# First keys gathered in four quadrants, their mask and weight applied behind the turn; GpSimd's set-up as scheduled tasks; the low weight bits extracted on ScalarE

## The chip, the cores and the metric

The program runs on one core of a Trainium2 chip. The metric is device time in microseconds (us) of one execution, the median of several runs. The engines are named as the profile names them: PE (TensorE: matmuls; PEld its weight loads), DVE (VectorE), ACT (ScalarE), POOL (GpSimd), SP (SyncE, which here only issues DMAs).

## The reference, cut to what matters

Linear attention with a delta rule over 768 tokens for 4 x 8 heads of 48, then two feed-forward layers over 3072 tokens. All in float32.

```python
k_n = k / (np.linalg.norm(k, axis=-1, keepdims=True) + 1e-06)
for t in range(S):                       # state: B, H, 48, 48
    y[:, :, t] = einsum('bhd,bhde->bhe', q[:, :, t], state)
    v_old = einsum('bhde,bhd->bhe', state, kt)
    state = state + bt[:, :, :, None] * einsum('bhd,bhe->bhde', kt, vt - v_old)
x = y.transpose(0, 2, 1, 3).reshape(3072, 384)
h = x @ w_in                             # 384 -> 2048
x = (h * sigmoid(1.702 * h)) @ w_out     # 2048 -> 384
p = domain_probs / domain_probs.sum(-1, keepdims=True)
out = sum(p[:, e:e+1] * (np.maximum(x @ w1[e], 0) @ w2[e]) for e in range(4))
```

## The kernel before, in words

**Attention.** The 768 steps are cut into 12 chunks u of 64 tokens. For a chunk all 32 heads lie in 16 groups g, two heads side by side (x = 0, 1) on the upper and lower half of the 128 partitions. Inside a chunk the recurrence becomes a triangular system in blocks of SB = 32 tokens: matmuls of the keys with themselves give `ps`; `keep_d` takes its diagonal blocks times a mask (and the rates beta) into `GG`, `keep_x` the blocks beside them into `G`. A triangular inverse is worked out for two chunks at a time (w = 0, 2, ..., 10): `begin` turns `GG` into `X` with a 32x32 transpose, `step(j)` eliminates column by column, `to_rows` turns it back. For w = 0 (`queue_first_inverse`) this is done on DVE, on two diagonal halves of 16 that `turn`, `first`, `out1`, `second`, `out2` join with matmuls; for all later w (`queue_inverse`) it is done on POOL. `queue_chain` then runs the chunk: `ks`, `rest`, `solve`, `cross`, `read` (the output y), `write` (the new state).

**First feed-forward layer.** The tokens are in 6 tiles t of 512; tile t needs chunks 2t and 2t+1. For each of 16 slices f of the hidden layer PE does 9 matmuls into `ph` (layer 1, L1013), ACT the gelu and its high part, DVE the low part `gh` (L1126), PE 9 matmuls into `px` (layer 2, L1108), one f later. The tiles 0 and 1 start in halves of 256 tokens. Weights and activations are split into a high and a low float32r part, so each product takes 3 matmuls. The weights w of this layer come as 64-bit numbers, and their float32 words are put together on chip in tile 0, per f: `small` (ACT L286), `low` (three low bits moved down, DVE L289), `shift` (DVE L293), `hi` (ACT L298), `lo` (DVE L301). Buffer `raw` or `rw` holds one f's words; PE waits for `wdone[f]` in tile 0.

**The second layers** (4 experts, L1013, L1235, L1265) follow from 613 us on; the change does not touch them.

**Order.** Each engine runs its instructions in the order in which the program was written out, and that order is made by a planner (`Order`, `Task`): every piece of the attention is a task with an engine, an estimated cost, dependencies and a priority; the planner keeps a clock for each engine (`od.clk`) and writes out a task when its estimate says that it is ready, between the matmuls of the feed-forward layer (`tick`). The estimate of a step of the inverse on POOL is `(0.52 + 0.0037 * m)` times 1.5 for w = 2, times 1.0 for later w. What really has to wait is ordered by semaphores; a wrong estimate makes an engine wait, or leaves a piece late. Before the first matmul of layer 1 only attention of chunk 0 and the first weights are there to do: a chain through all engines, called the start here.

**Set-up.** POOL writes masks (`gmask`, `cmask`, `pmask`, `hmask`) and zeros (`PQ`, `SU`, `stage`) ahead of all tasks, and the planner's clock of POOL starts at 9.5 us.

Of the kernel before, what the change touches and what calls it, by code (L numbers as in the profile page):

```python
# [9 lines left out]
I32 = mybir.dt.int32  # L10
AF = mybir.ActivationFunctionType
# [13 lines left out]
GW = 1  # L25
# [125 lines left out]
def delta_attention_moe_moe_kernel(  # L151
# [55 lines left out]
    cmask = ap_.tile([128, SB], F32, name="cmask")  # L207
# [43 lines left out]
    def queue_w1(f, after):  # L251
# [111 lines left out]
    NR = {}  # L363
# [88 lines left out]
    def queue_q(u):  # L452
# [8 lines left out]
        lq = task(load, "HW", 1.32, (edone.get(u - 2), normed[u] if u > 1 else None), lat=4.8, prio=p if u < 4 else p - 30, slack=5)  # L461
        ends, visits, masks = [], [], []
        whole = 1 if u < 2 else 2
        for o in range(2):
# [18 lines left out]
            if len(visits) == whole:  # L483
                t = task(lambda fs=tuple(visits): weave(fs), "PE", 1.0 if whole == 1 else 1.3,
                         (*placed[u], lq, begun[0], *(ends[-1:] if u > 1 else ())), prio=p + 1,
                         can=lambda: None if u > 1 and not od.moe else some_free(banks(), whole))
                for c, f in masks:
                    c.setdefault("end", []).append(task(f, "DVE", 0.6, (t,), prio=p + 1))
                    ends.append(c["end"][-1])
# [16 lines left out]
    def queue_premask(us):  # L506
# [11 lines left out]
        premasked[w] = task(premask, ("POOL", "DVE"), (1.2 * len(us), 0.6 * len(us)), (normed[w],), prio=p,  # L518
# [4 lines left out]
    def queue_g(u):  # L523
# [6 lines left out]
        whole = 1 if u < 4 else 2  # L530
        for o in range(2):
# [3 lines left out]
            def gram(o=o, cell=cell, flip=flip):  # L535
# [4 lines left out]
                for i in range(8):  # L540
                    g = 2 * i + o
                    if u < GW:
                        for x in range(2):
                            d, r = DR[x], TR[x]
                            mm(ps[r:r + C, i, :], lhsT=kr[d:d + D, g, :], rhs=kr[d:d + D, g, :], start=True, stop=True)
                            yield
                        continue
# [10 lines left out]
            def keep_d(x, o=o, cell=cell, flip=flip):  # L558
                if w not in GG:
                    GG[w] = scr[claim(SCR, gheld[w]["end"])][:, 0:2 * NP * SB].rearrange("p (g i) -> p g i", i=SB)  # L560
                a = rows(o)[0]
                if u < GW:
# [15 lines left out]
            halves.append((cell, gram, keep_d, keep_x))  # L578
# [5 lines left out]
            for hc, _, kd, kx in halves:  # L584
                parts = range(2) if whole == 2 and hc is not first else (None,)
                diag += [task(lambda kd=kd, x=x: kd(x), "DVE", 0.4 if u >= GW else 1.2, (a, premasked.get(w)), prio=p,
                              can=None if w or u or hc is not first else lambda: any_free(SCR)) for x in parts]
# [9 lines left out]
    def queue_inverse(us):  # L597
# [46 lines left out]
    def queue_first_inverse(us):  # L644
# [733 lines left out]
```

## Time and profile before

| | |
|---|---|
| median of 3 runs | 1409.41 us (1405.75 to 1409.59) |
| profiled execution | 1406.45 us, its span 1404.7 us |
| busy in the span | PE 1354.4 us (96%), DVE 617.5 (44%), ACT 421.2 (30%), POOL 202.5 (14%) |
| PE idle or waiting | mostly ahead of 66.4 us, where layer 1 starts, and in a few places up to 336 us |

The span is the time from the first to the last instruction of the program; 1.75 us of the profiled execution lie outside it. Shares of the whole span say little here: the start, tile 0, the step from tile 0 to tile 1 and the rest have different limits, so the profile is read by stretch.

### The profile page before, as it was taken

What the parts mean: (1) busy time and instruction counts of PE and PEld (TensorE: products, weight loads), DVE (VectorE), ACT (ScalarE), POOL (GpSimd) and SP (SyncE); (2) the same over time, 40 slices, a digit from 0 to 9 for tenths busy, and PEclk for the clock granted to TensorE, in tenths of its full rate; (3) what the DMA queues carried; (4) which work ended last, traced back from release to release, by engine and by line L of the source; (5) the groups of instructions that cost most, each with busy time, mean ns of one, the idle gap of its engine ahead of it and who ended that gap; (6) DMA issues with size and microseconds to landing.
All of it is one profiled execution on the core that took longest, in us unless ns stands there. A gap on an engine that the chain in (4) does not pass through costs nothing.

```text
span 1404.7 us, 29499 instructions
## 1 busy us (share of the span) xinstructions
PE 1354.4 (96%) x13072; PEld 1144.5 (81%) x13072; DVE 617.5 (44%) x1035; ACT 421.2 (30%) x797; POOL 202.5 (14%) x355
## 2 busy tenths in 40 slices
PE   5699999998999999999999999999999999999998
PEld 4588789986878788878888888888888888888888
DVE  7879466474363423323333224443233433233343
ACT  2564344352342434422222112222122222111111
POOL 3057543603507200000000000000000000000000
PEclk9999989999999999999999999999999999999999
DMA  8550131222020103201100001010001000011111
GB/s 222 171 173 17 28 96 40 61 62 61 12 61 7 39 5 134 68 0 29 33 30 30 8 1 30 31 38 31 1 19 30 31 31 8 0 30 31 31 30 46
DMA packets 53696, 63.39 MB, mean 45 GB/s; under 512 B 37120, under 2 KB 38592, under 8 KB 53568
## 3 DMA queue, kind: packets, MB, share of 16 engines
q1 hardware_dynamic: 53568, 61.50, 15.4%
q8 instruction: 102, 1.67, 0.5%
q14 instruction: 26, 0.21, 0.1%
HBM read 52.58 MB, written 7.91 MB: 43 GB/s over the span
## 4 chain that ended last, share of the span: by engine, by line
PE 92%; DVE 4%; issue 2%; DMA 1%; ACT 1%; SPq 0%; DVEq 0%; ACTq 0%
PE ph L1013 42%; PE po L1235 23%; PE px L1108 14%; PE po L1265 5%; PE y L849 2%; PE ch L820 1%; PE gp L550 1%; PE ch L806 1%; PE ch L872 1%; PE ch L835 1%; PE gp L473 1%; DMA rw<-in_w_dram 1%; DMA k<-in_k_dram 0%; ACT su L183 0%; DMA kt<-in_kt_dram 0%
## 5 line engine op out<-in xcount | busy, mean ns | idle before, releaser
L1013 PE MATMUL ph<-xs,w 128*128 128x512 f32 (+1 forms) x2808 | 657.5, 377 | 3.6 <-ACT xs L183 2.0
L1013 PEld LDWEIGHTS ph<-xs,w 128*128 128x128 f32 x2808 | 504.1, 190 | 96.7 <-ACT xs L183 2.1
L1296 DVE SCALAR_TENSOR_TENSOR hh<-ph,hh 128x512 fp32r<-128x512 f32 x192 | 132.5, 690 | 503.4 <-ACT hh L1295 503.4
L1235 PE MATMUL po<-hh,w 128*128 128x512 f32 x1440 | 352.4, 389 | 0.0
L1235 PEld LDWEIGHTS po<-hh,w 128*128 128x128 f32 x1440 | 270.4, 188 | 56.0
L1295 ACT ACTIVATE hh<-ph 128x512 fp32r<-128x512 f32 x192 | 114.9, 598 | 616.6 <-PE ph L1013 616.6
L1108 PE MATMUL px<-gh,w 128*128 128x512 f32 (+1 forms) x1080 | 231.6, 354 | 2.3 <-DVE gh L1126 2.1
L1108 PEld LDWEIGHTS px<-gh,w 128*128 128x128 f32 x1080 | 177.3, 190 | 30.4 <-DVE gh L1126 3.0
L1126 DVE TENSOR_TENSOR gh<-ph,gh 128x512 fp32r<-128x512 f32 (+1 forms) x120 | 69.9, 582 | 149.0 <-ACT gh L1125 147.8
L1123 ACT ACTIVATE ph<-ph 128x512 f32<-128x512 f32 (+1 forms) x120 | 59.6, 497 | 184.9 <-PE ph L1013 179.8
L621 POOL TENSOR_TENSOR scr<-scr,itmp 128x30 f32<-128x30 f32 (+9 forms) x150 | 85.0, 567 | 11.8
L619 POOL TENSOR_TENSOR itmp<-scr 128x30 f32<-128x30 f32 (+9 forms) x150 | 80.4, 536 | 11.1
L1265 PE MATMUL po<-w,hh 128*128 128x384 f32 x384 | 73.9, 342 | 0.0
L1265 PEld LDWEIGHTS po<-w,hh 128*128 128x128 f32 x384 | 69.3, 188 | 2.4
L1125 ACT CAST gh<-ph 128x512 fp32r<-128x512 f32 (+1 forms) x120 | 60.2, 502 | 3.8
L183 ACT COPY su<-ch 64x384 f32<-64x384 f32 (+2 forms) x85 | 38.1, 458 | 49.9 <-PE ch L820 48.5
L1095 DVE TENSOR_TENSOR xs<-x,xs 128x512 fp32r<-128x512 f32 x72 | 45.3, 684 | 0.0
L1094 ACT CAST xs<-x 128x512 fp32r<-128x512 f32 x72 | 39.7, 619 | 0.0
L813 DVE TENSOR_TENSOR v<-v,ch 128x384 f32<-128x384 f32 (+1 forms) x56 | 30.1, 551 | 17.5 <-PE ch L835 5.1
L478 DVE TENSOR_TENSOR pq<-gp,pmask 64x512 f32<-64x512 f32 x48 | 33.1, 689 | 5.9 <-PE gp L473 5.1
L243 DVE TENSOR_TENSOR w<-raw,w 128x768 fp32r<-128x768 f32 x32 | 30.7, 958 | 10.3 <-ACT w L242 9.5
L768 POOL TENSOR_TENSOR v<-v,nr 128x768 f32<-128x768 f32 x9 | 13.3, 1479 | 127.2 <-DMA v<-in_v_dram 119.1
(118 smaller groups left out, 765.8 us busy)
## 6 DMA issues: line engine op xcount, KB each, us to landing
raw<-in_we_dram SPq DMA_DIRECT2D x32, 384.0 KB, 3.0
rw<-in_w_dram SPq DMA_DIRECT2D x14, 768.0 KB, 5.7
raw<-prd SPq DMA_DIRECT2D x20, 256.0 KB, 3.2
kt<-in_kt_dram SPq DMA_DIRECT2D x24, 192.0 KB, 5.1
k<-in_k_dram SPq DMA_DIRECT2D x12, 384.0 KB, 6.1
pq<-in_q_dram SPq DMA_DIRECT2D x24, 192.0 KB, 4.2
v<-in_v_dram SPq DMA_DIRECT2D x12, 384.0 KB, 3.1
out_dram<-oacc SPq DMA_DIRECT2D x80, 48.0 KB, 1.7
```

The costliest lines, as they stand in the source:

```text
L619: E.tensor_tensor(out=tv, in0=x[:, j:j + 1, j + 1:].broadcast_to([128, m, r]), in1=x[:, 0:m, j:j + 1].broadcast_to([128, m, r]), op=ALU.mult)
L621: E.tensor_tensor(out=x[:, 0:m, j + 1:], in0=x[:, 0:m, j + 1:], in1=tv, op=ALU.add)
L1013: mm(ps, lhsT=w[:, a, kk * 128:(kk + 1) * 128], rhs=xs[kk][:, b, cs], start=kk == 0 and i == 0, stop=kk == KD - 1 and i == 2)
L1095: nc.vector.tensor_tensor(out=s[:, 1, :], in0=src, in1=s[:, 0, :].bitcast(F32), op=ALU.subtract)
L1108: mm(px[d][:, cs], lhsT=w[:, a, 384 + d * 128:384 + (d + 1) * 128], rhs=gh[:, b, 0:cs.stop - cs.start], start=f == 0 and i == 0 and cs.sta ...
L1123: a = task(lambda: nc.scalar.activation(out=ph, in_=ph, func=AF.Gelu_apprx_sigmoid), "ACT", 0.05 + 0.43 * c, (pe,), **kw)
L1125: a = task(lambda: nc.scalar.copy(out=hi, in_=ph), "ACT", 0.05 + 0.43 * c, (a,), **kw)
L1126: a = task(lambda: nc.vector.tensor_tensor(out=lo, in0=ph, in1=hi.bitcast(F32), op=ALU.subtract), "DVE", 0.07 + 0.53 * c, (a,), **kw)
L1235: mm(po[kk], lhsT=w[:, a, 384 + kk * 128:384 + (kk + 1) * 128], rhs=hh[:, c, :], start=f == 0 and i == 0, stop=f == F2 - 1 and i == 2)
L1265: mm(ps, lhsT=hh[:, a, b * 128:(b + 1) * 128], rhs=w[:, c, 384:768].rearrange("p (k a i) -> p a k i", a=4, k=KD), start=f == 0 and i == 0, ...
L1295: nc.scalar.activation(out=hh[:, 0, :], in_=ph, func=AF.Relu)
L1296: nc.vector.scalar_tensor_tensor(out=hh[:, 1, :], in0=ph, scalar=0.0, in1=hh[:, 0, :].bitcast(F32), op0=ALU.max, op1=ALU.subtract)
```

## The change

1. **Keys of chunks 0 and 1.** All chunks now gather their diagonal blocks by the same four kinds of matmul (32 rows each), so chunk 0 has 32 matmuls more, which are 64 in the profile's count, as a float32 product counts twice there. For w = 0 the diagonal blocks are copied as they are (`keep_raw`, ACT or DVE). The mask and the rates are applied behind the turn: POOL makes `m`, mask times rates, in two products (`weigh`), and `clear` multiplies by it, with one more memset. `cmask` goes.
2. **Set-up.** POOL's eight pieces become tasks of the planner in a new order (`j`, `q0`, `pm`, `h`, `su`, `st`, `q1`, `g`), and the DMAs of q wait for theirs only. The masks' sources lie in `spare`. On SP the loads of `raw` and of the first `rw` stood behind q of chunk 0 and of chunk 1, which both wait for POOL's zeros; now chunk 1's q stands behind these loads.
3. **Low bits.** `low` runs on ACT as an activation (a scaled copy between 32-bit integers) instead of DVE's shift: 16 instructions.
4. **Estimates.** A step of the inverse on POOL is estimated at 1.2 for w = 2 and 0.95 for later w; some others are changed in small ways. The order of all tasks is made anew.

```diff
-            nc.vector.tensor_scalar(out=cell["lo"], in0=cell["lo"], scalar1=29, scalar2=None,
-                                    op0=ALU.logical_shift_right)
+            nc.scalar.activation(out=cell["lo"].bitcast(U32), in_=cell["lo"].bitcast(U32), func=AF.Copy, scale=2.0 ** -29 * (1 - 2.0 ** -16),
+                                 bias=7.5 * 2.0 ** -16 - 0.5)
...
-            b = task(low, "DVE", 0.6, (dep, begun[0]), **kw)
+            b = task(low, "ACT", 0.9, (dep, begun[0]), **kw)
...
-                if u < GW:
-                    for r in range(0, 128, SB):
-                        V.tensor_tensor(out=GG[w][r:r + SB, o:NP:2, :] if not u else GG[w][r:r + SB, NP + o:2 * NP:2, :], in0=cell["ps"][r:r + SB, :, r % C:r % C + SB],
-                                        in1=cmask[r:r + SB].unsqueeze(1).broadcast_to([SB, 8, SB]), op=ALU.mult)
-                    return
...
+                copy(e, GG[w][r:r + n, c * NP + o:(c + 1) * NP:2, :], cell["ps"][s:s + n, :, a:a + SB])
...
-            last = task(lambda j=j: step(j), "POOL", (0.52 + 0.0037 * m) * (1.5 if w == 2 else 1.0), (last,), prio=p)
+            last = task(lambda j=j: step(j), "POOL", (0.52 + 0.0037 * m) * (1.2 if w == 2 else 0.95), (last,), prio=p)
...
+        def weigh(e):
+            bt = BT[w].rearrange("p (h i) -> p h i", h=2)
+            cell["m"] = spare[:, H * H:3 * H * H].rearrange("p (h a b) -> p h a b", h=2, a=H)
+            for h in range(2):
+                (V if e == "DVE" else nc.gpsimd).tensor_tensor(
+                    out=cell["m"][:, h], in0=jmask, in1=bt[:, h].unsqueeze(1).broadcast_to([128, H, H]), op=ALU.mult)
...
-            V.tensor_tensor(out=x, in0=x, in1=bt.unsqueeze(2).broadcast_to([128, 2, H, H]), op=ALU.mult)
+            V.tensor_tensor(out=x, in0=x, in1=cell["m"], op=ALU.mult)
             V.memset(X[w][:, H:, 0:H], 0.0)
+            V.memset(X[w][:, 0:H, H:], 0.0)
...
+        last = task(weigh, ("POOL", "DVE"), (1.2, 0.9), (normed[w], zeros["j"]), prio=0)
+        last = task(clear, "DVE", 1.4, (begun[w], last), prio=p)
```

What it does to the order is shown at three places. First DVE between the rates of chunks 0 and 1 (row `bt`, the reciprocal is ahead of it) and the first step of the inverse; `scr_99` before and `scr_98` after are `GG`, `scr_101` and `scr_100` are `X`. Before:

```order
20 L432 TENSOR_TENSOR bt<-bt,scr_98 128x32
21 L433 STREAM_TRANSPOSE bt<-bt 128x32
22 L564 TENSOR_TENSOR scr_99<-gp,cmask 32x8x32 x4
23 L571 TENSOR_TENSOR scr_99<-gp,cmask 128x8x32
24 L660 STREAM_TRANSPOSE scr_101<-scr_99 128x1024
25 L267 MEMSET rw 128x1
26 L666 TENSOR_TENSOR scr_101<-scr_101,bt 128x2x16x16
27 L667 MEMSET scr_101 128x16x16
28 L668 MEMSET scr_101 128x32
```

After:

```order
19 L433 TENSOR_TENSOR bt<-bt,scr_97 128x32
20 L434 STREAM_TRANSPOSE bt<-bt 128x32
21 L656 STREAM_TRANSPOSE scr_100<-scr_98 128x1024
22 L266 MEMSET rw 128x1
23 L668 TENSOR_TENSOR scr_100<-scr_100,sp 128x2x16x16
24 L669 MEMSET scr_100 128x16x16
25 L670 MEMSET scr_100 128x16x16
26 L671 MEMSET scr_100 128x32
```

The five masked products between the rates and the turn are gone (two plain copies stand further up, ahead of the second reduction), and one memset is new.

Second ACT from the first weights to the copy `out1` of the first inverse (`scr<-gp 128x16x16`), L286 before and L285 after being `small`, L288 after being `low`. Before:

```order
7 L286 ACTIVATE raw<-raw 128x768
8 L286 ACTIVATE rw<-rw 128x768 x3
9 L393 ACTIVATE scr_98<-k_2_83 128x768
10 L183 COPY scr_100<-gp 128x16x16
11 L286 ACTIVATE rw<-rw 128x768
12 L183 COPY su<-ch_593 32x4x48 x4
```

After:

```order
12 L288 ACTIVATE raw<-raw 128x768
13 L288 ACTIVATE rw<-rw 128x768
14 L285 ACTIVATE rw<-rw 128x768
15 L288 ACTIVATE rw<-rw 128x768
16 L285 ACTIVATE rw<-rw 128x768
17 L288 ACTIVATE rw<-rw 128x768
18 L394 ACTIVATE scr_97<-k_2_83 128x768
19 L183 COPY scr_99<-gp 128x16x16
```

Four activations for the low bits now stand ahead of the copy for which PE waits.

Third DVE around `to_rows` of w = 2 (`128x32x32`), which must wait for POOL; L571 before and L558 after are `keep_d` of w = 4, `gh` are the low parts of tile 0's gelu. Before:

```order
194 L1126 TENSOR_TENSOR gh<-ph,gh 128x512
195 L514 TENSOR_TENSOR scr_101<-gmask,bt 128x1024
196 L571 TENSOR_TENSOR scr_101<-gp,scr_101 128x8x32
197 L571 TENSOR_TENSOR scr_101<-gp,scr_101 64x8x32 x2
198 L183 COPY g<-gp 32x8x32
199 L1126 TENSOR_TENSOR gh<-ph,gh 128x512
200 L571 TENSOR_TENSOR scr_101<-gp,scr_101 128x8x32
201 L571 TENSOR_TENSOR scr_101<-gp,scr_101 64x8x32 x2
202 L610 STREAM_TRANSPOSE scr_99<-scr_101 128x1024
203 L1126 TENSOR_TENSOR gh<-ph,gh 128x512 x2
204 L642 STREAM_TRANSPOSE scr_98<-scr_98 128x32x32
```

After:

```order
175 L515 TENSOR_TENSOR scr_100<-gmask,bt 128x1024
176 L1139 TENSOR_TENSOR gh<-ph,gh 128x512
177 L558 TENSOR_TENSOR scr_100<-gp,scr_100 128x8x32
178 L558 TENSOR_TENSOR scr_100<-gp,scr_100 64x8x32 x2
179 L558 TENSOR_TENSOR scr_100<-gp,scr_100 128x8x32
180 L558 TENSOR_TENSOR scr_100<-gp,scr_100 64x8x32 x2
181 L1139 TENSOR_TENSOR gh<-ph,gh 128x512
182 L638 STREAM_TRANSPOSE scr_99<-scr_99 128x32x32
183 L606 STREAM_TRANSPOSE scr_98<-scr_100 128x1024
184 L1139 TENSOR_TENSOR gh<-ph,gh 128x512
```

Counted from the first `gh` of tile 0, `to_rows` of w = 2 stood behind the 21st and now stands behind the 18th of the tile's 24, still behind the `keep_d` of w = 4. With it chunk 2's chain moves: on PE its first matmuls (`ks`) stood behind 14 of tile 0's 16 f and now stand behind 11.

## Rows read from the trace of the kernel before

**Rows 1.** The page: busy time of each engine; DMA queues (packets, MB, share).

```profile
PE 1354.4 (96%) x13072; PEld 1144.5 (81%) x13072; DVE 617.5 (44%) x1035; ACT 421.2 (30%) x797; POOL 202.5 (14%) x355
...
q8 instruction: 102, 1.67, 0.5%
```

**Rows 2.** Busy by stretch: PE, PEld, DVE, ACT, POOL, clock, DMA, GB/s.

```profile
70.00:115.00 45.00, 43.89 (x1004) 40.03 (x1003) 36.15 (x59) 29.09 (x62) 27.61 (x37) 1.00 0.53 150
...
117.70:121.10 3.40, 3.40 (x18) 3.40 (x17) 3.40 (x5) 1.46 (x3) 3.17 (x4) 0.50 0.00 0
...
170.90:175.70 4.80, 1.45 (x70) 1.05 (x73) 1.66 (x3) 1.89 (x4) 4.29 (x7) 1.00 0.48 102
175.70:186.00 10.30, 9.40 (x232) 8.16 (x233) 4.54 (x8) 4.29 (x10) 9.06 (x15) 0.50 0.39 119
...
336.20:1404.70 1068.50, 1063.59 (x6581) 887.53 (x6580) 391.72 (x599) 272.33 (x474) 69.52 (x125) 1.00 0.10 29
```

**Rows 3.** Timeline of DVE in the start: start, duration, line, operation.

```profile
11.03 1.61 DVE L408 TENSOR_SCALAR scr<-scr 128x32 int32<-128x32 int32 x1
...
16.15 1.68 DVE L564 TENSOR_TENSOR scr<-gp,cmask 32x256 f32<-32x256 f32 x4
...
18.32 1.94 DVE L660 STREAM_TRANSPOSE scr<-scr 128x1024 f32<-128x1024 f32 x1
...
21.44 0.27 DVE L667 MEMSET scr<- 128x256 f32 x1
...
54.27 0.18 DVE L408 TENSOR_SCALAR scr<-scr 128x32 int32<-128x32 int32 x1
```

**Rows 4.** Timeline of POOL: last set-up piece; two steps and the end of w = 2.

```profile
10.80 1.81 POOL L1046 MEMSET pq<- 128x2048 f32 x1
...
93.76 1.11 POOL L619 TENSOR_TENSOR itmp<-scr 128x184 f32<-128x184 f32 x1
...
124.58 0.54 POOL L619 TENSOR_TENSOR itmp<-scr 128x184 f32<-128x184 f32 x1
...
132.75 1.92 POOL L625 TENSOR_TENSOR scr<-scr,bt 128x1024 f32<-128x1024 f32 x1
```

**Rows 5.** The chain of waits in the start: start, length, what.

```profile
33.22 1.94 PE gp L718 x128
...
36.19 0.61 PE gp L727 x29
36.80 2.73 issue
```

**Rows 6.** Timeline of SP's DMA queue in the start: start, duration, issues.

```profile
6.24 7.66 SPq L459 DMA_DIRECT2D pq<-in_q_dram  x4
...
14.62 0.43 SPq L277 DMA_DIRECT2D raw<-in_w_dram  x1
```

**Rows 7.** Timeline of ACT in the start; in brackets its idle time before, and why.

```profile
34.12 0.90 ACT L286 ACTIVATE rw<-rw 128x768 f32<-128x768 f32 x1 [0.97 <-DMA rw<-in_w_dram]
...
35.77 0.37 ACT L183 COPY scr<-gp 128x256 f32<-128x256 f32 x1
```

**Rows 8.** Groups by line, the low bits: busy us, mean ns of one | idle before.

```profile
L289 DVE TENSOR_SCALAR rw<-rw 128x768 int32<-128x768 int32 x14 | 9.8, 697 | 0.0
```

**Rows 9.** Timeline of PE in tile 0, around a wait for `gh`.

```profile
117.04 1.54 PE L1108 MATMUL px<-gh,w 128*128 128x256 f32 x8 [1.91 <-DVE gh L1126]
```

**Rows 10.** Timeline of DVE in tile 0: the 18th `gh`; `to_rows` of w = 2.

```profile
132.88 0.65 DVE L1126 TENSOR_TENSOR gh<-ph,gh 128x512 fp32r<-128x512 f32 x1
...
149.59 2.23 DVE L642 STREAM_TRANSPOSE scr<-scr 128x1024 f32<-128x1024 f32 x1
```

**Rows 11.** The chain of waits, later pieces.

```profile
111.24 0.58 DVE rw L289
...
174.27 2.33 DMA stage<-scr
...
325.93 4.84 issue
```

More of the change, by code (lines that the diff above doesn't have):

```diff
@@ L361, in delta_attention_moe_moe_kernel @@
     direct = {}
-    NR = {}
+    NR, zeros = {}, {}
+    spare = wp.tile([128, 1536], F32, name="sp", tag=f"w{RAW - 1}")
+    jmask = spare[:, 0:SB * SB // 4].rearrange("p (a b) -> p a b", a=SB // 2)
     def queue_keys(us):
@@ L487, in queue_q @@
                 for c, f in masks:
-                    c.setdefault("end", []).append(task(f, "DVE", 0.6, (t,), prio=p + 1))
+                    c.setdefault("end", []).append(task(f, "DVE", 0.69, (t, zeros["pm"]), prio=p + 1))
                     ends.append(c["end"][-1])
@@ L529, in queue_g @@
         diag, cross, halves, first = [], [], [], None
[L530 removed]
+        whole = 1 if u in (2, 3) else 2
         for o in range(2):
@@ L585, in queue_g @@
                 parts = range(2) if whole == 2 and hc is not first else (None,)
-                diag += [task(lambda kd=kd, x=x: kd(x), "DVE", 0.4 if u >= GW else 1.2, (a, premasked.get(w)), prio=p,
-                              can=None if w or u or hc is not first else lambda: any_free(SCR)) for x in parts]
+                diag += [task(lambda kd=kd, x=x: kd(x), "DVE", 0.4, (a, premasked.get(w)), prio=p) if w else
+                         task(lambda e, kd=kd, x=x: kd(e, x), ("ACT", "DVE"), (0.42, 0.42), (a,), prio=p,
+                              can=None if u or hc is not first else lambda: any_free(SCR)) for x in parts]
                 cross += [task(lambda e, x=x, kx=kx: kx(e, x), ("ACT", "DVE"), (0.3, 0.33), (a,), prio=p + 1)
@@ L689, in queue_first_inverse @@
                 marks.append(last)
-            last = task(lambda j=j: step(j), "DVE", 0.26 + 0.0042 * j * (H - 1 - j), (last,), prio=p)
+            last = task(lambda j=j: step(j), "DVE", 0.4 + 0.003 * j * (H - 1 - j), (last,), prio=p)
         last = task(end, "DVE", 0.6, (last,), prio=p)
@@ L746, in queue_first_inverse @@
                 a = task(lambda gn=gn, second=second: second(gn), "PE", 1.1 * n / NP, (a,), prio=p)
-            invdone[u] = task(out2, "DVE", 0.41, (a,), prio=p)
+            invdone[u] = task(out2, "DVE", 0.47, (a, *zeros.values()), prio=p)
             ends.append(invdone[u])
@@ L1039, in delta_attention_moe_moe_kernel @@
-        nc.gpsimd.memset(PQ[0], 0.0)
-        for r in range(0, 128, SB):
-            for o in range(2):
-                nc.gpsimd.affine_select(out=pmask[r:r + SB, o], in_=m2[r:r + SB], pattern=[[1, C]], compare_op=ALU.is_gt,
-                                        fill=0.0, base=-(r % C ^ SB * o), channel_multiplier=-1)
-        nc.gpsimd.memset(SU, 0.0)
-        nc.gpsimd.memset(stage, 0.0)
-        nc.gpsimd.memset(PQ[1], 0.0)
-        od.clk["POOL"] = 9.5
+        H = SB // 2
+        E_ = nc.gpsimd
@@ new lines, in delta_attention_moe_moe_kernel, with set_j, set_g @@
+        ones, minus = spare[:, 1024:1024 + C], spare[:, 1024 + C:1024 + C + SB]
+        def set_j():
+            E_.memset(minus, -1.0)
+            E_.affine_select(out=jmask, in_=minus[:, 0:1].unsqueeze(2).broadcast_to([128, H, H]), pattern=[[-1, H], [1, H]],
+                             compare_op=ALU.is_gt, fill=0.0, base=0, channel_multiplier=0)
+        def set_g():
+            for r in range(0, 128, SB):
+                at = slice(r, r + SB)
+                E_.affine_select(out=gmask[at], in_=minus[at], pattern=[[-1, SB]], compare_op=ALU.is_gt,
+                                 fill=0.0, base=0, channel_multiplier=1)
@@ new lines, in set_h, with set_p @@
+        def set_h():
+            E_.memset(hmask, -1.0)
+            for r in range(0, 128, SB):
+                at = slice(r, r + SB)
+                E_.affine_select(out=hmask[at], in_=hmask[at], pattern=[[0, 1]], compare_op=ALU.is_ge,
+                                 fill=0.0, base=H - 1, channel_multiplier=-1)
+        def set_p():
+            E_.memset(ones, 1.0)
+            for r in range(0, 128, SB):
+                for o in range(2):
+                    E_.affine_select(out=pmask[r:r + SB, o], in_=ones[r:r + SB], pattern=[[1, C]], compare_op=ALU.is_gt,
+                                     fill=0.0, base=-(r % C ^ SB * o), channel_multiplier=-1)
@@ L1050, in delta_attention_moe_moe_kernel @@
+        for n, fn, cost in (("j", set_j, 0.5), ("q0", lambda: E_.memset(PQ[0], 0.0), 1.85), ("pm", set_p, 1.95),
+                            ("h", set_h, 0.9), ("su", lambda: E_.memset(SU, 0.0), 1.4),
+                            ("st", lambda: E_.memset(stage, 0.0), 1.4), ("q1", lambda: E_.memset(PQ[1], 0.0), 1.85),
+                            ("g", set_g, 1.1)):
+            zeros[n] = task(fn, "POOL", cost, (), prio=2)
+        od.clk["POOL"] = 0.8
         loaded = queue_tile(0)
```

45 lines of the change are left out of this document (12 added, 33 removed).

## The prediction

> **What bounds the kernel now.** The first view is the page's busy time: PE is busy 96% of the span [rows 1]. The second is busy time by stretch: behind 336 us PE works 1063.59 of 1068.50 us at full clock [rows 2], so nothing that this change does there can shorten the run; it can only lose. What can be won lies before. There the chain of waits and the timelines, read one after the other, show four places where PE stands still for a cause that the change touches: the start, until layer 1 begins at 66.4; a stall in tile 0 that ends at 117.04; the step from tile 0 to tile 1 (170.9 to 186.0); and a pause at 325.93 in which PE waits for nothing that the profile shows. The reader should also see in [rows 2] what follows each stall: the granted clock is 0.50 in 117.7 to 121.1 and in 175.7 to 186.0, the lower of its two levels (1.2 of 2.4 GHz). PE had just stood still both times. Such a stretch costs half of its busy time on top of the stall, and both go together if the stall goes.
>
> **Term 1, from the rates to the turn: −3.3 us.** Behind the last operation on the rates DVE makes four masked products of 1.68 in all and a fifth, and the turn starts at 18.32 instead of 16.15 [rows 3]. The plain copies that replace them stand ahead of the rates, where DVE and ACT wait for keys anyway: −2.17. The first operation on the rates, L408, took 1.61, and 0.18 when it came again [rows 3]; it ended with POOL's last memset (10.80 + 1.81 = 12.61) [rows 4], so I read it as held up by POOL. In the changed order q1, that memset, is not the last piece, and the small selects of `g` stand behind it; POOL reaches them near 11: −1.43, and 0 if the hold stays. One memset of 0.27 is new. Sum −3.33; bounds −1.9 and −3.6 (the memset may overlap its neighbours). `weigh` needs the rates, as the turn does; it is two POOL products of 256 elements, and the nearest row is 1.92 for 1024 [rows 4], so about 0.5 each, 1.0 together. The turn's 1.94 [rows 3] hides it; without that cover it costs up to 1.0. The 64 extra matmuls stand in front of the turn, where PE then waits 11 us for it, and cost nothing.
>
> **Does the gain get through ACT?** The copy `out1`, for which PE's next matmuls wait, ran at 35.77, though PE was done at 33.22 + 1.94 = 35.16 [rows 5]: ACT came from `small`, which had waited for weights until 34.12 [rows 7]. If these weights come no earlier, two `low` of about 0.90 (the price of `small`, the same shape on the same engine, [rows 7]) put `out1` at about 36.7, and all of term 1 is lost. But the weights move. SP spent 7.66 us on four issues of q, as chunk 1's q waits for POOL's zeros until 12.61, and `raw` was issued only at 14.62 [rows 6]. Now `raw` and the first `rw` stand ahead of that wait and can go some 6 us earlier, and what follows them in the queue gains at least part of it. I take it that they land as much earlier as the turn ends.
>
> **Term 2, from the turn's end to `out2`: −1.0 us.** ACT's two extra `low` ahead of `out1` cost up to 1.8, about 0.6 beyond what the earlier weights give back. Against that stands the wait of 2.73 which came 29 matmuls into L727 [rows 5] and waits for no engine. The page gives its cause: 1.67 MB in 102 packets on the instruction queue, 16 KB each, against 2 x 13072 PE instructions [rows 1], 256 to a packet, or 128 matmuls with their weight loads. The boundary of such a block fell 29 into L727, with 128 matmuls of L718 just ahead that went by in 1.94 [rows 5]: too fast for the next block. With 64 more matmuls ahead, this boundary falls 29 + 128 − 64 = 93 into L718 (L722 now), and its block has PE's long wait for the turn to arrive in. The next falls 93 into L731, behind the wait for `out1`. If it is there in time, 2.73 goes; if it comes as late as now, nothing. I take 1.6 of it: −1.6 + 0.6 = −1.0, bounds −2.7 and +1.8. The Trainium skill (Runtime: NRT & Kernel Launch, section Instruction fetch mechanics) has the same blocks, 16 KiB of 256 instructions, and says that the next is fetched while the current one runs, so that the cost of a boundary is mostly hidden. By that rule the shift would give nothing and this term would be +0.6; the 2.73 in the trace speaks against it here.
>
> **Term 3, from `out2` to layer 1: 0.** DVE loses some six `low` of 0.70 [rows 8] and ACT gains as many of 0.90 [rows 7]. In this stretch the chain runs through ACT in its first half and through DVE in its second, so one loses what the other wins. Bounds −2 and +2 (three `low` on either).
>
> **Term 4, tile 0: −3.6 us.** PE waits 1.91 for `gh` [rows 9]. On the chain to it stand three `low`, of which [rows 11] has one; at 0.70 each [rows 8] they are 2.1 of DVE. Without them `gh` comes 2.1 earlier, and the stall is gone with the half-clock stretch behind it, 3.40 / 2 = 1.70 [rows 2]. −1.91 − 1.70 = −3.6; bound 0, where another piece fills DVE's time or ACT's hold the gelu up.
>
> **Term 5, from tile 0 to tile 1: −8.95 us.** `to_rows` of w = 2 ran on DVE at 149.59 [rows 10], though POOL had been done since 132.75 + 1.92 = 134.67 [rows 4]: the planner's factor of 1.5 had put it behind the 21st `gh`. Behind it came chunk 2's chain, whose `stage` transfer of 2.33 at 174.27 [rows 11] is what PE waited for. Of 170.9 to 175.7 PE used 1.45 of 4.80, and then it worked 9.40 of 10.30 at half clock [rows 2]. Lost: 4.80 − 1.45 = 3.35 and 10.30 − 9.40 / 2 = 5.60. In the changed order `to_rows` stands behind the 18th `gh`, which ran at 132.88 [rows 10] and would, moved by terms 1, 2 and 4, run near 125. Is POOL done by then? Two steps of the same 184 elements took 1.11 and 0.54 [rows 4]; the first met a `low` on DVE. Seven of them met POOL's inverse, so without them it should be shorter by some 7 x 0.57 = 4.0: 134.67 − 4.3 − 4.0 = 126.4. So DVE would wait about 1 us there at most, the 19th `gh` is still in time, and chunk 2's matmuls, behind 11 f instead of 14, come over 10 us earlier, where under 5 were missing. −8.95; bound 0.
>
> **Term 6, the pause at 325.93: 0.** 4.84 without a releaser [rows 11] has the look of the block wait of term 2, with some half-clock work behind it, which I put at the 1.7 of term 4. It comes where key loads burst into the DMA queues. In the changed order the matmuls on chunk keys shift against tile f's, and the blocks by 64 matmuls. Neither sign is likelier, so 0, with bounds of −6.5 and +6.5 (it goes, or a second one comes).
>
> **The sum.** −3.3 − 1.0 + 0 − 3.6 − 8.95 + 0 = −16.9. The profiled execution took 1406.45 (a span of 1404.7 and 1.75 outside): 1389.6. It lies 3.0 below the median of 1409.41; I add half of that, as the profile is one of the same spread: 1391.
>
> **The rivals.**
>
> *A. DVE stands in `to_rows` and waits for POOL.* All that DVE has behind it waits too: the transpose of the next `keep_d`, the 19th `gh`, and PE for that. If POOL gains nothing from the missing `low` it ends at 130.4, 5 us behind the 18th `gh`; with 2.23 for `to_rows` [rows 10] and as much for the transpose, the 19th `gh` comes some 3 us late: 3 + 1.7 of half clock, 4.7 in all. The next chunk's pieces move with it, and a second such stall is likely: 1396 with one, 1400 with two. For it: DVE's other operations of 768 elements hold POOL just as well, so POOL's gain is uncertain. Against it: two equal steps at 1.11 and 0.54.
>
> *B. ACT becomes the bound.* It gets 11 `low` of 0.90 in tile 0, where it was busy 29.09 of 45 [rows 2]; 10 us more make 39. A gelu behind them delays `ph` and `gh`, and each such stall costs, as at 117.04, 1.91 + 1.70 = 3.6. With terms 1, 2 and 5 at −13.3 the change loses from the fourth such stall on; with six, −13.3 + 21.6 = +8.3, near 1417. Against it: the average leaves ACT free a seventh of the time, and DVE is lighter by 0.70 for each.
>
> *C. The change does nothing that shows.* What the start and the steps give back is waited for elsewhere: the weights come no earlier (term 1 lost), POOL's chain sets chunk 2 as before, and a second block wait (+6.5) eats term 4 and a part of the rest: 1405 to 1413.
>
> *D. The rule of hidden block waits.* If the 2.73 has another cause that stays, only term 2 changes: −16.9 + 1.6 = −15.3, near 1392.5, inside the likeliest's range. By the Trainium skill's page named at term 2 this would be the time.
>
> **How the numbers follow.** The sum's way 0.48 and D with it 0.12, together the likeliest: 1391; its terms' bounds are mostly independent (term 6 is the widest), and its own range is 1383 to 1398. A 0.20, 1394 to 1405. C 0.12. B 0.08. From 1381 to 1407 leaves out B, most of C and a tail below: some 0.2. A difference under 0.3% (4.2 us) is about what cannot be told from no change here. Faster by more: the likeliest and most of A, 0.77; within: most of C and the rest of A, 0.14; slower: B and a little of C, 0.09.
>
> **What would show it in the profile after.** Term 1: L409 at 0.18, the turn near 15, `begin`'s multiply right behind it without a wait for POOL. Through ACT: `small` of the fourth weights near 31, `out1` within 1 us of PE's end. Term 2: no wait inside L731, or one at its 93rd matmul. Start as a whole: first `ph` 62 to 63. Term 4: no PE wait for `gh` near 110, no half-clock stretch. Term 5: `to_rows` of w = 2 near 127 with POOL done before it, PE without a gap or half clock between tiles 0 and 1. Term 6: where PE waits with no releaser behind 186. What would make the forecast wrong most: DVE standing in `to_rows` for POOL, ACT late with gelu, or a new pause like that of 325.93, with its half-clock stretch.

## The result and the profile after

The changed kernel takes 1387.4 us (1384.29 to 1390.42), the kernel before 1409.5: a ratio of 0.9848, interval 0.9819 to 0.9877. Two more series on other chips gave 0.9825 (0.9802 to 0.9849) and 0.9849 (0.9823 to 0.9875). The profiled execution took 1390.42, the slowest of its series, with a span of 1388.7.

The page and busy time by stretch, after (columns as in [rows 1, 2]):

```profile
PE 1344.4 (97%) x13136; PEld 1133.8 (82%) x13136; DVE 608.6 (44%) x1015; ACT 431.3 (31%) x811; POOL 206.5 (15%) x353
...
q8 instruction: 103, 1.69, 0.5%
```

```profile
70.00:115.00 45.00, 40.52 (x794) 36.62 (x793) 33.21 (x51) 30.10 (x59) 30.64 (x43) 0.96 0.43 124
...
167.00:190.00 23.00, 23.00 (x433) 20.70 (x432) 17.26 (x28) 11.39 (x27) 11.08 (x20) 1.00 0.58 144
```

The step from tile 0 to tile 1 has no gap and no half clock any more (23.00 of 23.00 at 1.00). But in the stretch 70 to 115 PE is busy for less time than in [rows 2]: 40.52 instead of 43.89.

The start, DVE, SP and ACT (timelines, as [rows 3, 6, 7]):

```profile
10.99 0.18 DVE L409 TENSOR_SCALAR scr<-scr 128x32 int32<-128x32 int32 x1
...
14.61 0.21 DVE L434 STREAM_TRANSPOSE bt<-bt 128x32 f32<-128x32 f32 x1
16.54 1.95 DVE L656 STREAM_TRANSPOSE scr<-scr 128x1024 f32<-128x1024 f32 x1 [1.72 <-ACT scr L183]
```

```profile
4.05 1.38 SPq L460 DMA_DIRECT2D pq<-in_q_dram  x2
...
6.16 1.26 SPq L276 DMA_DIRECT2D raw<-in_w_dram  x1
```

```profile
30.91 0.90 ACT L285 ACTIVATE rw<-rw 128x768 f32<-128x768 f32 x1
...
33.36 0.37 ACT L183 COPY scr<-gp 128x256 f32<-128x256 f32 x1
```

The rates end at 14.82, early as forecast, but DVE then waits 1.72 for ACT's copies of the keys, and the turn starts at 16.54. The weights come about 3 us earlier (`small` at 30.91 against 34.12) and `out1` 2.4 earlier (33.36 against 35.77). Why the copies are late is seen on PE, whose timeline and chain of waits follow (`issue` is time in which PE waits for nothing that the profile shows, called a wait without a releaser below):

```profile
14.60 0.21 PE L549 MATMUL gp<-kt 48*32 48x32 f32 x1 [5.11 <-issue]
```

```profile
33.78 1.46 PE gp L731 x93
35.24 1.50 issue
...
72.92 2.72 issue
```

PE waits 5.11 in the middle of chunk 1's keys with no releaser, 1.50 behind exactly the 93rd matmul of L731, and 2.72 at 72.92. The pause at 325.93 is gone. Tile 0 and the step (POOL and DVE timelines, PE's, SP's):

```profile
81.14 0.15 POOL L609 MEMSET scr<- 128x32 f32 x1 [23.48 <-DVE scr L606]
...
127.11 1.92 POOL L621 TENSOR_TENSOR scr<-scr,bt 128x1024 f32<-128x1024 f32 x1
```

```profile
132.64 0.69 DVE L1139 TENSOR_TENSOR gh<-ph,gh 128x512 fp32r<-128x512 f32 x1
133.25 2.20 DVE L638 STREAM_TRANSPOSE scr<-scr 128x1024 f32<-128x1024 f32 x1
```

```profile
105.79 1.22 PE L1121 MATMUL px<-gh,w 128*128 128x256 f32 x8 [1.11 <-DVE gh L1139]
```

```profile
154.26 4.10 SPq L979 DMA_DIRECT2D stage<-scr  x6
```

POOL ends at 129.03, `to_rows` runs at 133.25 right behind the 18th `gh`, and the `stage` transfers go out at 154 instead of around 172.

To see where time went, the losses of PE are summed by stretch of its own progress: idle time plus busy time times (1 − granted clock), over windows of 0.5 us. The start is the time of layer 1's tenth matmul; tile 0 goes to its 180th (12 of tile 0's 16 f), the step to its 288th (a quarter into tile 1), then come the stretch to the 648th, where tile 2 ends, and that to the end of the first feed-forward layer, behind the 1080th. What is left of the span, PE's work and some 3 to 4 us of idle time in the second layers, is 1310 to 1314 us in all kernels.

| kernel | start | tile 0 | step | to 648 | to the second layers | span |
|---|---|---|---|---|---|---|
| before | 68.9 | 5.8 | 9.7 | 8.4 | 0.9 | 1404.7 |
| changed, first profile | 63.6 | 7.7 | 0.1 | 5.8 | 1.1 | 1388.7 |
| changed, second (c0) | 63.3 | 2.1 | 0.1 | 2.2 | 1.1 | 1379.8 |
| changed, third (c1) | 63.2 | 3.2 | 0.1 | 5.7 | 1.0 | 1384.4 |

Between executions of one program it is waits without a releaser that come and go: at 72.92 and 207.67 in the first profile, neither in the second, at 203.27 alone in the third. With them come stretches of half clock (76.5 to 80.0 and 209.6 to 213.1 in the first profile). Another such stretch, where layer 1 begins, stands in the first and the third profile (62.9 to 66.3 and 61.9 to 65.4) and not in the second.

What these waits are can be read from the packets of the instruction queue, which the trace holds one by one: 16 KB each, a block of 128 matmuls with their weight loads. In the first profile one runs from 12.15 to 13.27, and PE goes on at 14.60; another from 34.33 to 35.26, and PE goes on at 36.74. In the kernel before one runs from 328.24 to 329.33, in the pause at 325.93, and PE goes on at 330.77. In all 14 profiles together some 90 waits without a releaser of 0.35 us or more stand where such a block ends in PE's program, about 128 matmuls apart, and each ends 1.2 to 1.6 us after a packet of this queue has landed. So PE waits for its own instructions there. (A wait of 0.70 or 0.71 us at L824, L820 before, stands in every kernel and is not one of them.)

### The profile page after: what moved, and what is told of

The parts are those of the page before. It is cut to its first block, busy times and chain, and to the rows that moved or that the text cites. A ratio compares the mean times of both kernels' runs of the same rounds, so it can differ in the third digit from the quotient of the medians.

```text
span 1388.7 us, 29634 instructions
## 1 busy us (share of the span) xinstructions
PE 1344.4 (97%) x13136; PEld 1133.8 (82%) x13136; DVE 608.6 (44%) x1015; ACT 431.3 (31%) x811; POOL 206.5 (15%) x353
## 4 chain that ended last, share of the span: by engine, by line
PE 94%; DVE 3%; issue 1%; DMA 1%; ACT 1%; SPq 0%; DVEq 0%; ACTq 0%
PE ph L1017 43%; PE po L1248 24%; PE px L1121 14%; PE po L1278 5%; PE y L853 2%; PE ch L824 1%; PE gp L545 1%; PE ch L810 1%; PE ch L876 1%; PE ch L839 1%; PE gp L474 1%; DMA kt<-in_kt_dram 1%; PE gp L549 0%; DVE rw L292 0%; DVE w L300 0%
## 5 line engine op out<-in xcount | busy, mean ns | idle before, releaser
L617 POOL TENSOR_TENSOR scr<-scr,itmp 128x30 f32<-128x30 f32 (+9 forms) x150 | 82.0, 547 | 11.8
L183 ACT COPY su<-ch 64x384 f32<-64x384 f32 (+2 forms) x77 | 34.2, 458 | 66.0 <-PE ch L824 64.9
L772 POOL TENSOR_TENSOR v<-v,nr 128x768 f32<-128x768 f32 x11 | 16.3, 1478 | 146.6 <-DMA v<-in_v_dram 136.0
```

Source lines behind the costliest of these rows:

```text
L617: E.tensor_tensor(out=x[:, 0:m, j + 1:], in0=x[:, 0:m, j + 1:], in1=tv, op=ALU.add)
```

## The experiments

My theory: three separate gains (start, tile 0, step), disturbed by waits on instruction blocks whose place is set by the count of matmuls and whose length is set by the DMA queues. The rivals: the gain is one edit's alone; or the waits without a releaser have another cause. Each kernel is timed against the kernel before on the same chip.

**The changed kernel again** (c0 with e1 to e3, c1 with e8 to e10).

> The changed kernel as it is, as the mark for the others of this chip: 1384 to 1390 us. If the waits on instruction blocks are set by where the blocks end in PE's program and by what the DMA queues hold, its PE waits stand at the same matmuls in this profile as in the first (one near 9.5 to 14.6 us, one at the 93rd matmul of L731, one near 73 us in L1121); if they are chance, they stand elsewhere.

> The changed kernel once more, as the mark for the next three on this chip: 1381 to 1390 us; PE's wait near 9.5 us and the one at the 93rd matmul of L731 stand where they stood twice, those near 73 and 208 us may be there or not.

The medians were 1384.19 and 1386.1 us. PE's wait near 9.5 us (4.84 and 3.83) and the one at the 93rd matmul of L731 (1.59 and 2.05) stood both times, the later ones varied as told above.

**e1: the low bits back on DVE.**

```diff
-            nc.scalar.activation(out=cell["lo"].bitcast(U32), ...)
+            nc.vector.tensor_scalar(out=cell["lo"], in0=cell["lo"], scalar1=29, scalar2=None, op0=ALU.logical_shift_right)
-            b = task(low, "ACT", 0.9, ...)
+            b = task(low, "DVE", 0.6, ...)
```

> The changed kernel with the low bits back on DVE. Mine: the stalls of PE for gh in tile 0 come back (2 to 4 us with their half clock), POOL's inverse of w = 2 takes about 50 us again instead of 47.9, and the time is 3 to 6 us above the changed kernel. Rival 1 (ACT was loaded just as badly, the move is neutral): within 2 us of it. Rival 2 (the whole gain of tile 0 and of the step to tile 1 comes from this move): 9 us or more above it.

The median was 1404.82, ratio 0.998 (0.9963 to 0.9997): 20 us above the changed kernel, so my 3 to 6 missed, and rival 2 is nearest by size. Its reason is not borne out. By stretch: start 66.2, tile 0 3.1, step 3.7, to 648 11.2, which against the changed kernel's second profile is 2.9, 1.0, 3.6 and 9.0 more; tile 0 and the step give 4.6 of these 16.5. This profile is the fastest of 12 executions (1399.22), so it lacks 5.6 of the 20. Some of the loss is waits on blocks (2.80 in the start; 0.70, 1.02 and 2.59 behind the step), which the new order places and the low bits do not. POOL's inverse took 51.2 us again, against 47.9 to 48.2 (I had expected about 50).

**e2: POOL's estimates back.** `(1.5 if w == 2 else 1.0)` in place of `(1.2 ... 0.95)`.

> The changed kernel with POOL's step estimated at 1.5 and 1.0 as before. Chunk 2's first matmuls stand behind 195 of layer 1's matmuls again (171 in the changed kernel, 198 before), to_rows of w = 2 behind the 20th gh. Mine: PE stands still again at the step from tile 0 to tile 1, with half clock behind it; 5 to 9 us above the changed kernel. Rival (the step was won by the earlier start and the lighter DVE, not by the estimates): within 2 us of it, no PE gap there.

The median was 1393.63, ratio 0.9905 (0.9876 to 0.9933): 9 us above the changed kernel. The gap is back, where 167 to 190 was full in the changed kernel:

```profile
160.00:182.00 22.00, 18.68 (x434) 15.70 (x435) 12.26 (x23) 10.60 (x24) 15.36 (x26) 0.84 0.46 115
```

Idle 3.3 and 18.7 x 0.16 = 3.0 of clock: 6.3 of the 9 lie here.

**e6, e7, e9, e10: the parts alone and in pairs**, by the same lines, from the kernel before (e6: estimates; e7: low bits on ACT; e9: both) or with both undone in the changed one (e10: keys and set-up only).

> The kernel before with the estimates of POOL's step at 1.2 and 0.95 alone: to_rows of w = 2 behind the 18th gh instead of the 21st, the low bits still on DVE. Mine: POOL ends near 134.7 as before, the 18th gh ran at 132.9, so DVE stands in to_rows for about 2 us, the 19th gh is late by 1 to 3 us, but the gap and the half clock at the step to tile 1 (8.9 us) go: 4 to 9 us faster than before. Rival A (standing in to_rows eats it): within 3 us of before. Rival (the estimates do nothing without the other parts): PE gap at 171 to 186 us still there.

> The kernel before with the low bits on ACT alone. Mine: the stall of 1.91 at 117 and its half clock go (-3.6), POOL's inverse is 2 us shorter, the step to tile 1 keeps its gap (to_rows behind the 21st gh as before), out1 in the start comes up to 1 us later: 1 to 4 us faster than before. Rival B (ACT becomes the bound): PE waits for gh or for xs behind ACT, and it is no faster or slower than before.

> The kernel before with the low bits on ACT and the estimates at 1.2 and 0.95, keys and set-up as before. By adding the two measured alone (-8.7 and +5.4): 3 us faster than before. Mine: the two need each other, as the low bits off DVE only pay when chunk 2's chain comes early, so that it is the changed kernel without the gain of its start (4.8): 14 to 19 us faster than before.

> The changed kernel with the low bits on DVE and the estimates at 1.5 and 1.0: only the first keys' copies and the set-up are changed. Mine: the start is 3 to 5 us shorter, the step to tile 1 keeps its gap and half clock, and a pause on an instruction block near 326 us may stand or not: 2 to 6 us faster than before. Rival (the early loads that come with the set-up's new order cost as much as they give): within 2 us of before.

| keys, set-up | low on ACT | estimates | ratio to before | start | tile 0 | step | to 648 |
|---|---|---|---|---|---|---|---|
| | | | 1 | 68.9 | 5.8 | 9.7 | 8.4 |
| | | e6 | 0.9938 (0.9918 to 0.9959) | 68.1 | 7.0 | 1.8 | 2.2 |
| | e7 | | 1.0038 (1.0020 to 1.0056) | 69.1 | 2.4 | 15.9 | 5.1 |
| | e9 | e9 | 0.9890 (0.9870 to 0.9910) | 72.1 | 2.3 | 0.1 | 2.2 |
| e10 | | | 1.0005 (0.9987 to 1.0022) | 66.7 | 4.5 | 17.3 | 2.8 |
| e2 | e2 | | 0.9905 (0.9876 to 0.9933) | 64.1 | 3.2 | 6.5 | 4.8 |
| e1 | | e1 | 0.9980 (0.9963 to 0.9997) | 66.2 | 3.1 | 3.7 | 11.2 |
| all | all | all | 0.9848 (0.9819 to 0.9877) | 63.6 | 7.7 | 0.1 | 5.8 |

The ratios are from all executions, the stretches from one profile each. The parts do not add: alone the low bits cost 0.4% (6 us more are lost at the step), with the estimates they give 0.5%, with keys and estimates 1.3%. Keys and set-up alone give nothing: 2 us at the start, 1 in tile 0 and 6 behind the step against 8 more at the step. Mine for e7 (1 to 4 us faster) and for e10 (2 to 6) were wrong; e10's rival (within 2 us of before) came true. For e6 (4 to 9) the ratio gives 8.7, and for e9 (14 to 19) 15.5, where adding e6 and e7 would give 3. The step shows why. In e7 POOL is done early, but `to_rows` still stands behind the 21st `gh`, where the old estimate put it (POOL and DVE timelines):

```profile
128.10 1.92 POOL L626 TENSOR_TENSOR scr<-scr,bt 128x1024 f32<-128x1024 f32 x1
```

```profile
146.13 2.24 DVE L643 STREAM_TRANSPOSE scr<-scr 128x1024 f32<-128x1024 f32 x1
```

Done at 130.02, used at 146.13. PE gets through tile 0 sooner: its last matmul of layer 1 there, the 216th, runs at 160.55 instead of 166.10, 5.5 earlier. Chunk 2's last `stage` transfer lands at 174.33 instead of 176.60, only 2.3 earlier. So PE stands longer between the two. In e6, the test of rival A, POOL is later than in the changed kernel, and still DVE doesn't stand, against my 2 us: between `gh` and `to_rows` it has other work (the rows are POOL's end, then DVE):

```profile
133.57 1.92 POOL L625 TENSOR_TENSOR scr<-scr,bt 128x1024 f32<-128x1024 f32 x1
```

```profile
133.70 0.65 DVE L1126 TENSOR_TENSOR gh<-ph,gh 128x512 fp32r<-128x512 f32 x1
134.27 2.31 DVE L514 TENSOR_TENSOR scr<-gmask,bt 128x1024 f32<-128x1024 f32 x1
136.50 2.19 DVE L642 STREAM_TRANSPOSE scr<-scr 128x1024 f32<-128x1024 f32 x1
```

**e4, e5: the block ends moved.** Some of chunk 1's q matmuls are made twice while PE waits for the turn; the order is the same on all engines. The edit of e4 follows; e5 has `u == 1 and not o` in place of `u == 1`.

```diff
-                        mm(ps[r:r + C, i, :], lhsT=kr[d:d + D, g, :], rhs=pq[d:d + D, g, x, :], start=True, stop=True)
+                        for _ in range(2 if u == 1 else 1):
+                            mm(ps[r:r + C, i, :], lhsT=kr[d:d + D, g, :], rhs=pq[d:d + D, g, x, :], start=True, stop=True)
```

> The changed kernel with 32 matmuls of chunk 1's q product made twice (64 in the profile's count, written to the same place with the same result), in the time in which PE waits for the turn anyway; all engines' orders are otherwise the same. If PE's waits without a releaser are block ends every 128 matmuls: the wait inside L731 moves from its 93rd matmul to its 29th, as in the kernel before, and is about 2.7 instead of 1.5 us; the waits near 73 us and near 208 us move by 64 matmuls or go; the time moves by -5 to +5 us against the changed kernel with no other cause. If they have another cause: the wait stays at the 93rd matmul and the time within 1 us.

> As with 64, but 16 matmuls doubled (32 in the profile's count). By the block ends: the wait inside L731 stands at its 61st matmul, between 1.5 and 2.7 us long; the later waits move by 32 matmuls, which can hide or open one: -5 to +5 us. By another cause: nothing moves.

The chain of waits of e4, then e5 (their L732 is L731):

```profile
33.67 0.61 PE gp L732 x29
34.28 2.50 issue
```

```profile
35.69 1.03 PE gp L732 x61
36.73 0.85 issue
```

The wait moved to the 29th and to the 61st matmul, as the block ends say; another cause is out for this one. Its length does not follow its place alone (2.50, 0.85, 1.50 at the 93rd). In e4 the later block ends cost too (its chain of waits again):

```profile
47.43 1.47 issue
...
51.55 2.45 issue
...
63.74 1.51 issue
```

Layer 1 starts at 65.44 there and at 63.18 in e5, where the changed kernel's three profiles have 59.42 to 60.74 and the kernel before 66.39. With the same order and other block ends, 2 to 6 us of the start's gain are gone. The times, 1387.79 (0.9872, 0.9843 to 0.9901) and 1388.13 (0.9866, 0.9839 to 0.9893), can't be told one by one from the changed kernel's three series (0.9825 to 0.9849), but they, e3 and e8 all lie above them.

**e3 and e8: the wait of 5 us at 9.5.** e3 holds v and the first weights back behind chunk 1's q; the planner then changes the order on DVE, ACT and POOL as well. e8 puts small matmuls ahead of the first keys, which was meant to bring PE into the second block before the loads queue up; the rest of its order is the same.

```diff
e3
+        if f < 2:
+            after = (*after, zeros["q1"])
-        dep = task(load, "HW", ..., lat=3.0, prio=50)
+        dep = task(load, "HW", ..., lat=3.0, prio=50 if f > 1 else 9)
-        lv = task(load_v, "HW", 0.65, (*before, normed[u] if u else None), ...)
+        lv = task(load_v, "HW", 0.65, (*before, normed[u] if u else zeros["q1"]), ...)
e8
+        def ahead():
+            t = bank([128, 8, C], ())
+            for _ in range(47):
+                mm(t[0:SB, 0, 0:2], lhsT=minus[0:SB, 0:SB], rhs=minus[0:SB, 0:2], start=True, stop=True)
+        task(ahead, "PE", 0.5, (zeros["j"],), prio=0)
```

> The changed kernel with v and the first two loads of weights held back until POOL has set the second PQ, so that chunk 1's q stands ahead of them on SP as it did before. If PE's 5.16 us wait at 9.45 is an instruction block queued behind q, v and the weights on the DMA engines: the wait shrinks by 1.5 us or more, the turn starts near 15 instead of 16.54, and against it the weights land later, so the first matmul of layer 1 comes between 1.5 us earlier and 1 us later than 62.2. If the wait has to do with keys or with PE itself: it stays at 5 us and the turn at 16.5.

> The changed kernel with 94 small matmuls (in the profile's count) ahead of the first keys, while PE has nothing to do; their results are overwritten. All else is in the same order. If PE's wait of 5 us at 9.5 is the second instruction block, asked for too late and queued behind the loads: PE enters that block before the keys land, the wait goes, the turn starts near 14.9 instead of 16.3 to 16.5, and the block ends move by 94, to the first matmuls of L722 and L731, where a wait of 1 to 3 us may stand instead of 1.5 at the 93rd: 0 to 2 us faster than the changed kernel. If the wait has another cause: it stays, and the turn too.

What the DMA engines do while PE waits, 9 to 15 us, in the kernel before, the changed one and e3 (the last two columns are DMA share and GB/s):

```profile
9.00:15.00 6.00, 6.00 (x148) 5.54 (x140) 5.39 (x16) 3.03 (x7) 3.61 (x3) 1.00 0.49 69
```

```profile
9.00:15.00 6.00, 0.89 (x68) 0.72 (x58) 4.27 (x17) 2.30 (x5) 2.70 (x7) 1.00 1.13 302
```

```profile
9.00:15.00 6.00, 1.99 (x112) 1.65 (x108) 3.92 (x17) 2.48 (x6) 2.68 (x6) 1.00 0.85 131
```

In e3 the wait is 4.01 and the turn starts at 15.98. That is 1.1 less than in the first profile, under the 1.5 I asked for, and the changed kernel's own three profiles spread further (3.83 to 5.11). So e3 does not show that v and the weights hold the block back. Nor does the rate alone set the wait: it was 3.83 in the third profile of the changed kernel, at 344 GB/s, and 4.01 in e3, at 131. What can be seen is that the block comes late in every kernel with the new set-up (3.40 to 5.25) and in none with the old one (e6, e7, e9). PE runs the first matmul of the block before it at 6.06 in the first profile, and the packet starts 6.09 us after that; in the kernel before it starts 1.24 us after that (9.33). PE also needs its block sooner now, 3.15 us after entering the one before instead of 5.65. That keys and chunk 0's q, which the set-up's new order sends 2.2 us earlier (4.05 against 6.24), are what the packet queues behind is argued, not shown. What late weights cost stands in e3 beside another block wait (ACT's timeline, then PE's):

```profile
33.69 0.88 ACT L285 ACTIVATE rw<-rw 128x768 f32<-128x768 f32 x1
...
35.98 0.37 ACT L183 COPY scr<-gp 128x256 f32<-128x256 f32 x1 [0.61 <-ACT rw L288]
```

```profile
35.19 0.71 PE L724 MATMUL gp<-scr,scr 32*32 32x16 f32 x35 [2.38 <-issue]
```

`out1` runs at 35.98 instead of 33.36. ACT was done with the second of these weights' `low` at 35.37, PE, behind its wait of 2.38, at 35.90; so either alone would have made it 2 us or more late. The time was 1389.59 (0.986, 0.9834 to 0.9887). In e8 (DVE's timeline, then PE's) the turn no longer waits:

```profile
14.86 0.21 DVE L434 STREAM_TRANSPOSE bt<-bt 128x32 f32<-128x32 f32 x1
14.99 1.92 DVE L656 STREAM_TRANSPOSE scr<-scr 128x1024 f32<-128x1024 f32 x1
```

```profile
11.61 0.33 PE L545 MATMUL gp<-kt 48*32 48x64 f32 x4 [3.40 <-issue]
...
35.70 0.23 PE L722 MATMUL gp<-scr,scr 32*32 32x16 f32 x2 [3.17 <-issue]
...
39.42 0.24 PE L731 MATMUL gp<-scr,scr 32*32 32x16 f32 x2 [1.10 <-issue]
```

Against what I expected, the wait itself did not go: it is 3.40 and ends at 11.61, early enough for the copies. PE did not enter the block before it any earlier (6.21, 6.06 in the changed kernel), and still its packet came at 8.67 instead of 12.15; why is open. The 1.5 won at the turn is lost at the block ends, which now fall into L722 and L731, on the path: 3.17 and 1.10. Layer 1 starts at 65.92. (In c1 the first wait happened to be 3.83 and its turn came at 14.93, so beside that execution nothing is won.) The time was 1389.43 (0.987, 0.9847 to 0.9892). No kernel of this study beat the changed one.

## Why the prediction was right, step by step

**Size.** 1391 was forecast, 1387.4 measured, within the likeliest case's own range. The step to tile 1, half of the sum, came by the mechanism forecast. In the start the sum came out right in part by luck, through block waits that the prediction had not counted.

**Term 1 (−3.3).** The steps were right: L409 took 0.18, the products are gone, the rates end 1.4 earlier, and where the block comes soon enough (e8) the turn starts at 14.99, 3.33 before 18.32. In the changed kernel 1.6 of it is lost, as the copies of the keys, which I put "where DVE and ACT wait for keys anyway", come late behind PE's 5.11: measured −1.78 (−2.05 and −3.39 in the other two profiles). That PE's next block could come too late behind the new set-up was the step I missed. The 64 extra matmuls, which I had put at no cost, have a part in it: in the kernel before the same block begins in q (L473, at 14.98), behind all keys, and now it begins among chunk 1's keys, on the path to the turn. I put it down to the earlier loads, the weights' among them, which I had counted only as a gain; e3 does not settle it.

**Through ACT and term 2 (−1.0).** `out2` on DVE's timeline, before and after:

```profile
41.22 0.48 DVE L732 SCALAR_TENSOR_TENSOR scr<-gp,hmask,scr 128x256 f32<-128x256 f32 x1 [1.99 <-PE gp L727]
```

```profile
37.58 0.48 DVE L736 SCALAR_TENSOR_TENSOR scr<-gp,hmask,scr 128x256 f32<-128x256 f32 x1 [0.69 <-PE gp L731]
```

From the turn's end (33.07 before, 31.20 after) to its start 8.15 became 6.38, −1.8, inside the bounds. `small` ran 3.2 earlier (30.91, against 34.12 [rows 7]), so `out1` came 0.5 nearer to the turn's end instead of 0.6 further from it. The wait stood at the 93rd matmul of L731 as worked out, and was 1.50, so 1.2 was won there instead of 1.6. Rival D falls: the wait is a block's, as e4, e5 and the packets show. The Trainium skill (Runtime: NRT & Kernel Launch, section Instruction fetch mechanics) gives a block 256 instructions, has the next fetched while the current one runs, and calls the cost of a boundary mostly hidden. The trace agrees on the size (103 packets for 2 x 13136 instructions), and by count on the rest: of some hundred boundaries in the first profile, four cost over 0.35 us. But these four cost 1.5 to 5.1 us each.

**Term 3 (0).** From `out2` to layer 1's first matmul on the chain (62.22 against 67.05): 25.8 became 24.6, −1.2, within its bounds, but by luck. The kernel before has three block waits on its chain of waits here, which the prediction left out:

```profile
42.65 0.45 issue
...
47.45 0.48 issue
...
54.02 1.63 issue
```

The changed kernel has none on its chain. Without them the stretch became 1.4 longer (23.3 to 24.6), so it is not shown that ACT and DVE gave and took alike. Terms 1 to 3 together: −4.8, forecast −4.3. Of the −4.8 block waits on the chain make up 3.8 (5.29 before, 1.50 after), where term 2 had put 1.6. They hang on where blocks end in PE's program: in e4, with the same order, they add up to 8.8 and layer 1 starts only 0.95 earlier than in the kernel before.

**Term 4 (−3.6).** The stall of 1.91 became one of 1.11 without half clock. Tile 0 lost 5.8 before, and 2.1 and 3.2 in the profiles where no block wait of over 0.35 us falls into it: −2.6 to −3.7. In the first profile the block wait at 72.92 cost more than the term gave (7.7).

**Term 5 (−8.95).** −9.6. In the kernel before POOL's inverse began here (POOL's timeline) and ended at 134.67 [rows 4], 50.1 in all:

```profile
84.60 0.16 POOL L613 MEMSET scr<- 128x32 f32 x1 [21.64 <-DVE scr L610]
```

It became shorter by 2.2 (129.03 − 81.14 = 47.9), not by 4.0. The step of 1.11 from which the 4.0 was worked out ran from 93.76, and beside it DVE had not only `low` but `shift` (L293, 93.53 to 94.49), which stayed on DVE. DVE still did not stand: the 18th `gh` ran at 132.64 and not near 125, with the block wait at 72.92 ahead of it, and in the other two profiles `to_rows` ran at 127.76 and 128.85, where POOL had been done since 124.05 and 125.05. e2 and e6 show that the place of `to_rows` does it: undone alone it costs 6.4 at the step, done alone it wins 7.9 there. Rival A did not come, not in e6 either, where POOL ended 1.1 us behind the 18th `gh`. Rival B neither: in 70 to 115 ACT was busy 30.10 instead of 29.09 of 45. Only six `low` fell into tile 0, 5.5 us, not eleven, and the copies of the next keys (six of `g`) came later than this stretch.

**Term 6 (0).** Wrong as a value: of 8.4 lost up to the 648th matmul, 2.2 to 5.8 are left, as the pause at 325.93 went and a shorter one (1.98 at 207.67) comes in some executions. That pause comes back in e1, and there it can be read (windows, then PE's timeline):

```profile
325.70:329.70 4.00, 3.96 (x154) 3.15 (x135) 3.08 (x5) 2.16 (x6) 0.00 (x0) 1.00 1.11 247
329.70:332.20 2.50, 0.00 (x0) 0.00 (x0) 1.33 (x2) 0.36 (x1) 1.44 (x6) 0.92 1.05 252
332.20:336.00 3.80, 3.75 (x52) 3.18 (x52) 2.11 (x4) 0.00 (x0) 3.17 (x9) 0.50 0.12 35
```

```profile
332.25 1.55 PE L474 MATMUL gp<-pq,kt 48*64 48x64 f32 x47 [2.59 <-issue]
```

PE makes 154 matmuls in 4 us while key loads fill the DMA engines, then it stands with the DMA share still at 1.05, then it works at half clock: a fast run of small matmuls meets a burst of loads. That both pauses are waits on a block is shown by the packets (in e1 one ran from 329.63 to 330.69, and PE went on at 332.25). That the pause is gone in the changed kernel because its order keeps the two apart is argued, not shown.

**What stays open.** Why the low bits on DVE cost 20 us in e1 is known by stretch and not piece by piece, since the planner's whole order differs. The start of e9 is 3.1 longer than before; the block waits of over 0.35 us between its turn and layer 1 add up to 9.2 us against 6.5 before, which is most of it. What in the new set-up holds back the block near 9.5 us is not settled, nor which of two executions gets a block wait (72.92, 207.67).

## What to carry to other kernels

Where a planner's estimates fix the order, a faster operation brings nothing until the estimate follows: the low bits alone made the kernel slower, the estimate alone gave 0.6%, all together 1.5%. Test such edits in pairs as well as singly. When loads are sent earlier, ask whether the instruction stream still comes in time, and where in a run of small matmuls a block of it ends. A gain of a few us in such a run may be no more than a shift of block ends: move them, by doubling a few matmuls off the path, before you believe in it.

## What the runs showed of the hardware that was not expected

Where PE waits for nothing that the profile names, a packet of the instruction queue had landed 1.2 to 1.6 us before PE went on, in some 90 waits of 14 profiles. Such a packet started 6.09 us after PE had entered the block before it in the changed kernel's start (302 GB/s on the DMA engines), and 1.24 us after in the kernel before (69 GB/s). The first cost PE 5.11 us, the second nothing, as PE also took longer over its block then (5.65 us against 3.15). A wait on a block keeps its place in the program when the program is run again. When 32 or 64 matmuls are put ahead of it, it falls on a matmul that many places earlier in the old order. Its length does not repeat (3.83, 4.84 and 5.11 at the same matmul).
